# Windowed attention by quarters: 192 score columns a head in place of 256

## The chip, the cores and the metric

The kernel runs on one core of one Trainium2 chip. The metric is the device time of one execution in microseconds (us). Work is spread over TensorE (PE, with its weight loads shown apart as PEld), VectorE (DVE), ScalarE (ACT), GpSimd (POOL) and the DMA queues that SP, ACT and POOL issue to.

## The reference

Attention with a sliding window of 128 keys and 4 sink keys, for 4 batches, 8 heads, 768 positions and head size 64; its output, laid out as 3072 tokens by 512, goes through a highway layer.

```python
pos = np.arange(S)
is_sink = pos[None, :] < int(n_sink)                 # 4
rel = pos[:, None] - pos[None, :]
in_window = (rel >= 0) & (rel < int(window))         # 128
scores = np.where(is_sink | in_window, q @ k.T / sqrt(D), -1e9)
a = softmax(scores)
x = (a @ v) laid out as [3072, 512]
H = np.maximum(x @ w_h, 0.0)
T = 1.0 / (1.0 + np.exp(-(x @ w_t + b_t)))
out = T * H + (1.0 - T) * x
```

A query sees its own key and the 127 before it, and always the first 4 keys of its batch.

## The kernel before

The 3072 tokens are 24 blocks of 128, six to a batch (`NSC` = 6), and each block n goes through a chain of small steps. The order of all steps is written out by hand in `_STEPS`, as `name:block`, and every engine runs its instructions in that order. `_FILLM` puts so many half-size warm-up matmuls ahead of some early steps.

The steps of one block:

- `lq`, `lk`, `lv` (lines 152 to 171): loads of queries, keys and values by POOL's DMA queue, cast from fp32 to fp16 on the way. Blocks 0 to 5 (`PACKED`) load q and k two tokens to a row, into one tile `sp`; the others load plainly, into `qsd` and `ksd`. `v_all` holds the values of block n in 65 columns a head, the last one set to 1, so that the row sums come out of the same matmul.
- `T` (lines 270 to 294): transposes q and k on TensorE, 64 rows at a time; 32 transposes of 64 by 64 for a packed block (line 281), 16 of 64 by 128 for the others (line 291). `cT` copies the result to `qk` on ScalarE (lines 299 and 302).
- `S0`, `S1` (`scores`, line 346): scores of the heads 0 to 3 and 4 to 7, keys on the partitions. For each head there are two matmuls, the 128 keys of the block before and the 128 of its own, against 128 queries: 256 columns a head, or 128 in the first block of a batch. The two heads of a pair lie in the row halves 0-63 and 64-127 and write two different PSUM banks (`sps[:, hh]`).
- `E0`, `E1` (`expo`, line 354): exponential on ScalarE, 1024 columns at a time. `M0`, `M1` (`masked`, line 365): multiplication with a 0/1 mask on VectorE, which brings in the window.
- `sk`, `es`, `BA` (lines 326, 331, 375 and 378): scores of the sink keys, their exponential, and their part of the output. A `sk` serves two blocks. `BA:n` also starts the gate's sum of block n-1 with its bias. Blocks 0 and 1 of a batch have no such step, because the sink keys lie in the window's two key blocks, and their masks (`mask0`, `mask1`) let them through.
- `AV` (line 398): 16 matmuls of 128 keys by 128 queries by 66 columns (8 in a batch's first block), summed in `av`, one PSUM bank for four heads.
- `rec`, `x` (lines 407 and 412): division by the row sums, on VectorE. `X` (line 423) and `cX` (line 434): transposes of the result on TensorE and the copy on ScalarE. `X` uses the PSUM buffer of `av`.
- `Tt`, `u`, `g` (lines 443 to 472): the gate, four matmuls of 512 columns, tanh and scaling. `H`, `d` (lines 459 and 465): the other branch. `ee`, `o` (lines 478 and 484): the mix, and the store by SP's queue.

The last block (`LB`) is done in two halves, with steps named `AVa`, `AVb`, `Xa` and so on (lines 487 to 567). `pks` (line 306) puts the sink keys and values of a batch in place on POOL; `lsv` loads the latter by SP's queue. `pi` and `pm` make the identity and the masks on POOL, and `K0` to `K6` other constants on VectorE.

Of the kernel before, what the change touches and what calls it, by code (L numbers as in the profile page):

```python
# [8 lines left out]
FP16 = mybir.dt.float16  # L9
FP32 = mybir.dt.float32  # L10
AF = mybir.ActivationFunctionType
# [8 lines left out]
_FILL = {'T:5': 1}  # L20
_FILLM = {'T:0': 5, 'T:1': 4, 'S0:0': 1, 'T:2': 9, 'S0:1': 8, 'S1:1': 1, 'AV:0': 1, 'S0:2': 2, 'T:4': 5, 'X:0': 3, 'AV:1': 1, 'S0:3': 2}
_STEPS = """
    K4:0 lq:0 K6:0 lk:0 lk:1 lq:1 K0:0 lk:2 lq:2 pi:0 K3:0 lv:0 lk:4 T:0 cT:0 T:1 pm:0 cT:1
    lsv:0 S0:0 lv:1 lq:4 T:2 K1:0 lk:3 K5:0 lq:3 E0:0 cT:2 S1:0 M0:0 E1:0 S0:1 lw_t:0 lv:2 S1:1
    lbt:0 M1:0 AV:0 E0:1 M0:1 S0:2 E1:1 rec:0 E0:2 K2:0 T:4 x:0 lw_h:0 pks:0 X:0 T:3 cT:4 cX:0
    S1:2 lq:5 lk:5 lv:3 lv:4 lk:6 M1:1 AV:1 rec:1 cT:3 E1:2 x:1 lq:6 S0:3 lq:8 lk:7 lq:7 lk:8
    lv:5 E0:3 sk:2 lk:9 lv:6 lv:7 X:1 sv:0 cX:1 M0:2 M1:2 S1:3 es:2 Tt:0 AV:2 M0:3 BA:2 E1:3
    u:0 S1:4 rec:2 x:2 g:0 S0:4 M1:3 lq:9 Tt:1 H:0 E1:4 X:2 u:1 T:5 E0:4 g:1 H:1 cX:2 cT:5 AV:3
    lk:14 S0:5 d:0 BA:3 M1:4 ee:0 o:0 Tt:2 lk:10 E0:5 u:2 d:1 sk:4 es:4 rec:3 x:3 T:6 X:3 cX:3
    M0:4 cT:6 lv:9 ee:1 S1:5 H:2 AV:4 M0:5 E1:5 BA:4 d:2 S0:6 rec:4 g:2 Tt:3 T:7 x:4 E0:6 o:1  # L30
    M1:5 lsv:6 ee:2 u:3 X:4 cX:4 cT:7 S1:6 H:3 g:3 E1:6 M0:6 AV:5 lq:11 lq:10 S0:7 BA:5 d:3
    E0:7 T:8 cT:8 rec:5 Tt:4 ee:3 S1:7 x:5 X:5 u:4 H:4 cX:5 lv:8 M0:7 M1:6 S0:8 pks:6 lk:11
    lq:12 o:3 lk:12 lv:11 d:4 E1:7 AV:6 E0:8 rec:6 sv:6 Tt:5 x:6 M1:7 T:9 X:6 S1:8 u:5 cX:6 o:2
    g:5 H:5 cT:9 g:4 AV:7 E1:8 S0:9 Tt:6 E0:9 d:5 rec:7 u:6 sk:8 M0:8 T:10 x:7 ee:4 ee:5 M1:8
    X:7 S1:9 es:8 cX:7 g:6 cT:10 H:6 o:4 lv:10 d:6 AV:8 BA:8 S0:10 rec:8 x:8 Tt:7 E1:9 M1:9
    T:11 E0:10 X:8 S1:10 M0:9 H:7 ee:6 u:7 cX:8 cT:11 E1:10 AV:9 o:5 M0:10 BA:9 rec:9 S0:11 d:7
    Tt:8 g:7 sk:10 x:9 E0:11 u:8 T:12 S1:11 X:9 M1:10 M0:11 es:10 cX:9 H:8 cT:12 o:6 AV:10
    E1:11 d:8 BA:10 S0:12 E0:12 rec:10 g:8 x:10 Tt:9 lv:12 lq:13 lk:13 ee:8 M1:11 ee:7 lq:15
    T:13 o:8 X:10 S1:12 H:9 d:9 lq:14 u:9 cX:10 AV:11 lsv:12 lv:13 BA:11 rec:11 cT:13 g:9 lq:18
    x:11 lk:15 E1:12 S0:13 Tt:10 pks:12 lv:14 o:7 lk:16 X:11 ee:9 T:14 M1:12 E0:13 M0:12 M0:13  # L40
    S1:13 u:10 sv:12 cX:11 cT:14 E1:13 H:10 AV:12 rec:12 S0:14 Tt:11 g:10 x:12 lq:16 d:10 M1:13
    X:12 lk:17 E0:14 lq:17 M0:14 T:15 o:9 lv:15 u:11 cX:12 cT:15 S1:14 E1:14 H:11 d:11 AV:13
    rec:13 ee:10 S0:15 g:11 Tt:12 sk:14 x:13 M1:14 T:16 E0:15 lsv:18 u:12 o:10 X:13 S1:15 ee:11
    M0:15 es:14 H:12 o:11 cX:13 AV:14 BA:14 cT:16 rec:14 S0:16 lk:18 E1:15 Tt:13 g:12 E0:16
    T:17 x:14 X:14 d:12 lv:16 u:13 cX:14 S1:16 H:13 M1:15 g:13 M0:16 AV:15 d:13 cT:17 BA:15
    rec:15 E1:16 ee:13 x:15 o:13 ee:12 M1:16 S0:17 E0:17 Tt:14 u:14 o:12 sk:16 T:18 X:15 es:16
    S1:17 lk:19 H:14 lk:20 cX:15 lq:19 AV:16 d:14 lq:21 lv:17 BA:16 cT:18 lq:20 E1:17 lv:18
    rec:16 S0:18 g:14 Tt:15 x:16 M1:17 lk:21 M0:17 E0:18 T:19 pks:18 X:16 u:15 cX:16 S1:18 H:15
    cT:19 M0:18 AV:17 E1:18 BA:17 S0:19 Tt:16 E0:19 sv:18 u:16 lv:19 d:15 rec:17 ee:14 T:20
    lk:22 x:17 M1:18 X:17 g:15 o:14 ee:15 cX:17 H:16 S1:19 g:16 d:16 AV:18 rec:18 lq:22 lv:20  # L50
    lq:23 lv:21 lk:23 lv:22 ee:16 cT:20 E1:19 S0:20 x:18 M1:19 E0:20 Tt:17 T:21 u:17 X:18 cX:18
    M0:19 cT:21 S1:20 H:17 M0:20 o:16 lv:23 AV:19 E1:20 S0:21 Tt:18 d:17 E0:21 sk:20 rec:19
    g:17 x:19 X:19 o:15 u:18 M1:20 M0:21 ee:17 es:20 cX:19 T:22 S1:21 H:18 AV:20 BA:20 d:18
    cT:22 S0:22 Tt:19 g:18 E1:21 E0:22 S1:22 rec:20 ee:18 x:20 M1:21 o:17 M0:22 u:19 X:20 T:23
    cX:20 H:19 g:19 cT:23 d:19 E1:22 AV:21 BA:21 Tt:20 rec:21 sk:22 ee:19 u:20 x:21 es:22 S1:23
    M1:22 o:19 X:21 H:20 cX:21 AV:22 o:18 BA:22 d:20 S0:23 rec:22 E1:23 E0:23 Tt:21 g:20 x:22
    u:21 M1:23 X:22 M0:23 cX:22 ee:20 H:21 d:21 BA:23 AVa:23 AVb:23 Tt:22 g:21 u:22 reca:23
    ee:21 H:22 recb:23 xa:23 xb:23 o:21 Xa:23 g:22 cXa:23 Xb:23 d:22 o:20 cXb:23 TA:23 HA:23
    ee:22 Ta:23 o:22 Hb:23 ua:23 Tb:23 db:23 ga:23 ub:23 Ha:23 da:23 gb:23 eea:23 eeb:23 oa:23
    ob:23  # L60
# [4 lines left out]
def kernel(  # L65
# [31 lines left out]
    VW = H * 65 + 8  # L97
# [14 lines left out]
    NV = NB  # L112
    PACKED = (0, 1, 2, 3, 4, 5)
# [3 lines left out]
    mask = const.tile([P, 2, P], FP16, tag="mask", name="mask")  # L117
    mask0 = const.tile([P, P], FP16, tag="mask0", name="mask0")
    mask1 = const.tile([P, 2, P], FP16, tag="mask1", name="mask1")
# [17 lines left out]
    LB = NB - 1  # L137
# [14 lines left out]
    def load(x, n):  # L152
        if (x, n) in f32:
            eng = nc.sync if x == "q" else nc.scalar
            eng.dma_start(out=f32[x, n], in_=dram(x, n))
        elif x == "v":
            vt = v_all[:, n, :]
            nc.gpsimd.dma_start(  # L158
                out=vt[:, 0:H * 65].rearrange("p (h e) -> p h e", e=65)[:, :, 0:D], in_=dram(x, n))
        elif n in PACKED:  # L160
            if n not in sd_of:
                sd_of[n] = const.tile([P, H, 2 * D], FP16, tag=f"sp{n}", name=f"sp{n}")
            b, c = divmod(n, NSC)
            src = {"q": q, "k": k}[x][b, :, c * P:(c + 1) * P, :]
            i = "qk".index(x)
            nc.gpsimd.dma_start(out=sd_of[n][64 * i:64 * i + 64],
                                in_=src.rearrange("h (p t) d -> p h (t d)", t=2))
        else:
            sd = sd_pool.tile([P, H, D], FP16, tag=f"{x}sd", name=f"{x}sd")
            nc.gpsimd.dma_start(out=sd, in_=dram(x, n))  # L170
            sd_of[x, n] = sd

    def v_cols(n, h):
        return v_all[:, n, 65 * h:65 * h + _AVN]
# [20 lines left out]
    def first():  # L195
        nc.vector.memset(warm, 0.0)  # L196
        nc.vector.memset(ident, 1.0)
        nc.vector.memset(mask, 1.0)
        v_ones(0, NSC)
        warm_up(16)  # L200

    def v_ones(a, b):
        nc.vector.memset(v_all[:, a:b, 0:H * 65].rearrange("p t (h e) -> p t h e", e=65)[:, :, :, D:D + 1], 1.0)
        nc.vector.memset(v_all[:, a:b, H * 65:VW], 0.0)

# [5 lines left out]
    def pm():  # L211
        nc.gpsimd.affine_select(
            out=mask[:, 1, :], in_=mask[:, 1, :], compare_op=ALU.is_ge, fill=0.0,
            base=0, pattern=[[1, P]], channel_multiplier=-1)
        nc.gpsimd.affine_select(
            out=mask[:, 0, :], in_=mask[:, 0, :], compare_op=ALU.is_ge, fill=0.0,
            base=-1, pattern=[[-1, P]], channel_multiplier=1)

    def K1():
        nc.vector.tensor_copy(out=mask0, in_=mask[:, 1, :])  # L220
        nc.vector.memset(mask0[0:NSINK, :], 1.0)
        nc.vector.tensor_copy(out=mask1, in_=mask)
        nc.vector.memset(mask1[0:NSINK, 0, :], 1.0)
# [21 lines left out]
    def K4():  # L245
        v_ones(NSC, NB)
# [21 lines left out]
    avt = {}  # L268

    def T(n):  # L270
        tpf = s_ps.tile([P, 2, DM], FP32, tag="s", name="tp")
        tp = tpf.bitcast(FP16)
        if n in PACKED:
            sd = sd_of.pop(n)
            for j in range(NHP):
                for t in range(2):
                    o = (2 * j + t) * 64
                    for hh in range(2):
                        for i in range(2):
                            rows = slice(64 * i, 64 * i + 64)  # L280
                            nc.tensor.transpose(tp[64 * hh:64 * hh + 64, i, o:o + 64],  # L281
                                                sd[rows, 2 * j + hh, t * D:(t + 1) * D],
                                                ident[rows, rows])
        else:
            qsd, ksd = sd_of.pop(("q", n)), sd_of.pop(("k", n))
            for i, sd in enumerate((qsd, ksd)):
                for j in range(NHP):
                    for a in range(2):
                        rows = slice(64 * a, 64 * a + 64)
                        o = (i * NHP + j) * 64  # L290
                        nc.tensor.transpose(tp[:, a, o:o + 64], sd[rows, 2 * j:2 * j + 2, :],  # L291
                                            ident[rows, rows])
        tp_of[n] = tp

    def cT(n):
        qk = qkT_pool.tile([P, 2 * NHP, P], FP16, tag="qk", name="qk")
        src = tp_of.pop(n)[:, :, 0:DM]
        if n in PACKED:
# [330 lines left out]
```

## Time and profile before

| | |
|---|---|
| median of 3 runs | 114.89 us (114.72 to 117.13) |
| the profiled execution | 114.55 us |
| its span in the profile | 112.5 us |
| TensorE busy | 101.1 us, 1730 matmuls |
| VectorE busy | 94.3 us |
| ScalarE busy | 93.4 us |
| POOL busy | 67.8 us |
| granted TensorE clock, mean | 0.991 |
| loads by POOL's queue | 69792 packets, 10.49 MB |

The span is what the profiler recorded from the first to the last instruction; the time of the execution is 2.05 us longer. Busy time of TensorE is modelled, since its matmuls overlap. A group's line gives the line of the code, the engine, what it writes and reads, the number of instructions, their busy time and the mean duration of one in ns; durations overlap where an engine pipelines, so that a matmul lasts 200 to 400 ns in the records while the next one starts some 30 to 220 ns later.

### The profile page before, as it was taken

To read this page: it belongs to the slowest core of one execution; us is meant where nothing else is said; L and a number is where in the kernel's file an instruction comes from. 1 tells how busy PE (TensorE), PEld (TensorE's weight loads), DVE (VectorE), ACT (ScalarE), POOL (GpSimd) and SP (SyncE) were. 2 spreads that over 40 slices of the span, in tenths; PEclk is the share of its full clock that TensorE was granted. 3 is DMA by queue.
4 is the path that set the end of the run, shared out by engine and by line. 5 is a ranking of instruction groups with operands and counts; after the bars stand their busy time and mean duration, and the time that the engine had idled before them with its cause. 6 is when DMAs were issued, how large, how long until landed. Compare 5 with 4: busy or idle time off the path is not lost.

```text
span 112.5 us, 4097 instructions
## 1 busy us (share of the span) xinstructions
PE 101.1 (90%) x1730; PEld 58.5 (52%) x1730; DVE 94.3 (84%) x225; ACT 93.4 (83%) x131; POOL 67.8 (60%) x93
## 2 busy tenths in 40 slices
PE   5859988979799999999999989999999999999820
PEld 2334555635466555575555546656655666454510
DVE  4314448688589999999999999999999999999980
ACT  4049999978699999999999999999999999783320
POOL 6999996569699599991105999965994000000000
PEclk9999999999999999999999999999999999999996
DMA  0999999999999999999932999999999950240242
GB/s 0 130 150 145 156 162 195 176 154 151 198 160 188 165 176 181 159 207 194 207 116 96 83 166 167 227 192 155 261 160 204 196 136 11 90 187 0 93 187 93
DMA packets 73573, 17.07 MB, mean 152 GB/s; under 512 B 69330, under 2 KB 70610, under 8 KB 73556
## 3 DMA queue, kind: packets, MB, share of 16 engines
q0 software_dynamic: 69792, 10.49, 133.3%
q1 hardware_dynamic: 3620, 6.20, 15.2%
q8 instruction: 13, 0.21, 0.8%
q10 hardware_dynamic: 144, 0.13, 0.3%
q14 instruction: 4, 0.03, 0.1%
HBM read 21.01 MB, written 6.29 MB: 243 GB/s over the span
## 4 chain that ended last, share of the span: by engine, by line
PE 56%; ACT 8%; DVE 1%; issue 1%; DVEq 0%; ACTq 0%
PE hps L459 15%; PE tps L446 13%; PE sps L346 7%; PE av L398 6%; ACT e L354 4%; PE tp L291 4%; PE tps L375 2%; ACT qk L302 2%; PE xtp L423 2%; PE sk L326 1%; PE av L378 1%; ACT u L451 1%; PE tps L443 1%; PE lts L541 1%; PE av L494 1%
## 5 line engine op out<-in xcount | busy, mean ns | idle before, releaser
L354 ACT ACTIVATE e<-sps 128x1024 f16<-128x1024 f32 (+1 forms) x48 | 44.7, 984 | 1.3 <-PE sps L346 1.2
L365 DVE TENSOR_TENSOR e<-e,mask 128x1024 f16<-128x1024 f16 (+1 forms) x48 | 29.4, 635 | 3.0 <-ACT e L354 3.0
L459 PE MATMUL hps<-wh_sb,xT 128*128 128x512 f16 x92 | 23.8, 381 | 0.0
L446 PE MATMUL tps<-wt_sb,xT 128*128 128x512 f16 x92 | 23.8, 381 | 0.0
L158 POOL DMA_DIRECT2D v_all<-in_v_dram x24 | 21.9, 917 | 1.3 <-DMA qsd<-in_q_dram 1.0
L346 PE MATMUL sps<-qk 64*128 64x128 f16 x352 | 17.9, 217 | 1.0 <-ACT qk L299 0.8
L302 ACT COPY qk<-tp 128x1024 f16<-128x1024 f16 x18 | 18.7, 1037 | 0.0
L170 POOL DMA_DIRECT2D ksd<-in_k_dram x18 | 16.5, 926 | 2.2 <-DMA wh_sb<-in_moe_w_h_dram 2.0
L465 DVE SCALAR_TENSOR_TENSOR dd<-hps,xh 128x512 f16<-128x512 f32 x23 | 15.6, 680 | 1.6 <-PE hps L459 1.4
L170 POOL DMA_DIRECT2D qsd<-in_q_dram x18 | 16.3, 914 | 1.2 <-DMA wt_sb<-in_moe_w_t_dram 1.0
L451 ACT ACTIVATE u<-tps 128x512 f16<-128x512 f32 x23 | 14.2, 620 | 3.2 <-PE tps L446 3.1
L412 DVE TENSOR_TENSOR xh<-av,rec 128x512 f16<-128x512 f32 x23 | 15.7, 681 | 0.1
L398 PEld LDWEIGHTS <-e 128*128 128x128 f16 x336 | 13.2, 97 | 4.8 <-DVE e L365 0.6
L484 DVE TENSOR_TENSOR otok<-xh,ee 128x512 f32<-128x512 f16 x23 | 15.6, 681 | 0.1
L346 PEld LDWEIGHTS <-qk 64*128 64x128 f16 x352 | 12.8, 94 | 4.6 <-issue 3.4
L434 ACT COPY xT<-xtp 128x512 f16<-128x512 f16 x23 | 13.7, 598 | 1.3 <-PE xtp L423 1.2
L398 PE MATMUL av<-v_all,e 128*128 128x66 f16 x336 | 14.2, 194 | 0.0
L299 ACT COPY qk<-tp 128x1024 f16<-128x1024 f16 x6 | 7.9, 1317 | 5.7 <-PE tp L281 5.6
L446 PEld LDWEIGHTS <-xT 128*128 128x128 f16 x92 | 7.7, 97 | 8.1 <-issue 0.6
L459 PEld LDWEIGHTS <-xT 128*128 128x128 f16 x92 | 7.2, 98 | 8.0 <-DMA wh_sb<-in_moe_w_h_dram 0.5
L264 PE MATMUL wps<-warm 128*128 128x512 f16 (+1 forms) x33 | 9.9, 414 | 1.3 <-DVE warm L196 1.3
L478 DVE TENSOR_TENSOR ee<-gt,dd 128x512 f16<-128x512 f16 x23 | 9.3, 409 | 0.0
(75 smaller groups left out, 110.4 us busy)
## 6 DMA issues: line engine op xcount, KB each, us to landing
out_dram<-otok SPq DMA_DIRECT2D x23, 256.0 KB, 4.9
v_all<-in_v_dram POOLq DMA_DIRECT2D x24, 128.0 KB, 7.1
ksd<-in_k_dram POOLq DMA_DIRECT2D x18, 128.0 KB, 7.3
qsd<-in_q_dram POOLq DMA_DIRECT2D x18, 128.0 KB, 7.0
sp<-in_q_dram POOLq DMA_DIRECT2D x6, 128.0 KB, 4.6
sp<-in_k_dram POOLq DMA_DIRECT2D x6, 128.0 KB, 4.8
wt_sb<-in_moe_w_t_dram POOLq DMA_DIRECT2D x1, 512.0 KB, 8.4
wh_sb<-in_moe_w_h_dram POOLq DMA_DIRECT2D x1, 512.0 KB, 10.1
```

What stands on the lines that cost most here:

```text
L158: nc.gpsimd.dma_start(out=vt[:, 0:H * 65].rearrange("p (h e) -> p h e", e=65)[:, :, 0:D], in_=dram(x, n))
L170: nc.gpsimd.dma_start(out=sd, in_=dram(x, n))
L302: nc.scalar.copy(out=qk.rearrange("p j (a t) -> p a j t", a=2), in_=src.rearrange("p a (j t) -> p a j t", t=64))
L346: nc.tensor.matmul(sps[:, hh, o:o + P], lhsT=kk[rows, hp, :], rhs=qT[rows, hp, :], start=True, stop=True)
L354: nc.scalar.activation(out=e.rearrange("p a b c d -> p a (b c d)"), in_=sps[:, :, 0:2 * np_ * P], func=AF.Exp, bias=_EXP_BIAS, scale=SCALE)
L365: nc.vector.tensor_tensor(out=ev, in0=ev, in1=m.unsqueeze(1).to_broadcast([P, 4, np_ * P]), op=ALU.mult)
L398: nc.tensor.matmul(av[:, g, 2 * hl + hh, 0:_AVN], lhsT=e[:, hh, hl, pc, :], rhs=v_cols(m, h), start=fresh, stop=False, skip_group_check=True)
L412: nc.vector.tensor_tensor(out=xh.rearrange("p (h d) -> p h d", d=D), in0=av_of.pop(n)[:, :, 0:D], in1=rec_of.pop(n).unsqueeze(2).to_broadc ...
L446: nc.tensor.matmul(t_of[n], lhsT=xT[:, kc, :], rhs=wt_sb[:, kc, :], start=False, stop=(kc == NOC - 1), skip_group_check=True)
L459: nc.tensor.matmul(hps, lhsT=xT[:, kc, :], rhs=wh_sb[:, kc, :], start=(kc == 0), stop=(kc == NOC - 1))
L465: nc.vector.scalar_tensor_tensor(out=dd, in0=h_of.pop(n), scalar=0.0, in1=xh_of[n], op0=ALU.max, op1=ALU.subtract)
L484: eng.tensor_tensor(out=otok, in0=xh_of.pop(n), in1=ee_of.pop(n), op=ALU.add)
```

## The change

A query in the first half of its block sees the keys from 127 before it up to itself. Cut into quarters of 64 keys by 64 queries, two of the eight quarters of a head are masked as a whole: the first 64 keys of the block before against the second 64 queries, and the second 64 keys of the own block against the first 64 queries. The change leaves these out.

- Scores: the 128 columns that all queries need hold the last 64 keys of the block before (partitions 0-63) and the first 64 of the own block (64-127). 64 more columns hold the two triangles: the last 64 own keys by the last 64 queries (0-63), and the first 64 keys of the block before by the first 64 queries (64-127). Each part is a matmul of its own with 64 keys as its stationary operand: 16 for four heads in place of 8. The exponential and the mask have 768 columns in place of 1024.
- Values: `lv` loads windows that are shifted by 64 tokens, 7 a batch (28 in all), the first and the last of half size; 80 columns a head. `AV` becomes 8 matmuls of the full shape, and the triangles are a step of their own, `AX`, with 16 matmuls of 64 keys by 64 queries, which go from one row half to the other output half.
- Sinks: the triangle no longer holds the sink keys for the second half of block 1, so block 1 of each batch gets a `BA` too; there are three `sk` and `es` a batch (the last for one block) in place of two.
- Loads: q and k of blocks 0 to 5 are loaded and transposed as those of the others. `PACKED` is gone.
- Masks: 192 columns, made by four selects on POOL in place of two.
- The order of all steps and the warm-up matmuls are written anew.

The core of the diff:

```diff
-_FILLM = {'T:0': 5, 'T:1': 4, 'S0:0': 1, 'T:2': 9, 'S0:1': 8, 'S1:1': 1, 'AV:0': 1, 'S0:2': 2, 'T:4': 5, 'X:0': 3, 'AV:1': 1, 'S0:3': 2}
+_FILLM = {'T:0': 15, 'S1:0': 10, 'T:1': 4, 'S0:1': 8, 'T:2': 3, 'AX:0': 2, 'S1:2': 2, 'S0:2': 4, 'T:3': 3, 'sk:1': 4}
 _STEPS = """
...
+    lq:1 lq:0 lk:0 lv:0 pi:0 T:0 K4:0 lk:1 lq:2 K6:0 pm:0 lk:2 cT:0 K0:0 lsv:6 S1:0 lbt:0 K1:0
...
+    cX:3 T:6 lv:14 lv:6 H:2 cT:6 lq:8 M0:4 S1:5 M0:5 BA:4 ee:1 lk:13 d:2 Tt:3 AV:4 lk:9 AX:4
...
         elif x == "v":
+            b, j = divmod(n, NW)
+            lo, hi = max(0, j * P - 64), min(S, j * P + 64)
+            r0 = lo - (j * P - 64)
+            vt = v_all[r0:r0 + hi - lo, n, :]
+            nc.gpsimd.dma_start(out=vt.rearrange("p (h e) -> p h e", e=VP)[:, :, 0:D],
+                                in_=v[b, :, lo:hi, :].transpose([1, 0, 2]))
...
     def scores(n, g):
         qT, kT = qkT[n]
-        srcs = ([] if n % NSC == 0 else [qkT[n - 1][1]]) + [kT]
-        np_ = len(srcs)
         sps = s_ps.tile([P, 2, 512], FP32, tag="s", name="sps")
+        if n % NSC == 0:
+            w, parts = P, [(0, kT, 64, 0, 0, P), (64, kT, 0, 0, 0, P)]
+        else:
+            kp = qkT[n - 1][1]
+            w, parts = 192, [(0, kp, 64, 0, 0, P), (64, kT, 0, 0, 0, P),
+                             (0, kT, 64, P, 64, 64), (64, kp, 0, P, 0, 64)]
         for hl in range(2):
             hp = 2 * g + hl
-            for pc, kk in enumerate(srcs):
+            for c0, kk, k0, o, q0, nq in parts:
                 for hh in range(2):
                     rows = slice(64 * hh, 64 * hh + 64)
-                    o = (hl * np_ + pc) * P
-                    nc.tensor.matmul(sps[:, hh, o:o + P], lhsT=kk[rows, hp, :],
-                                     rhs=qT[rows, hp, :], start=True, stop=True)
+                    nc.tensor.matmul(sps[c0:c0 + 64, hh, hl * w + o:hl * w + o + nq],
+                                     lhsT=kk[rows, hp, k0:k0 + 64], rhs=qT[rows, hp, q0:q0 + nq],
+                                     start=True, stop=True)
...
+    def av_full(n, g):
...
+        for hl in range(2):
+            for hh in range(2):
+                nc.tensor.matmul(
+                    av[:, g, 2 * hl + hh, 0:_AVN], lhsT=e[:, hh, hl, 0:P],
+                    rhs=v_cols(v_slot(n, 0), 2 * (2 * g + hl) + hh), start=fresh, stop=False,
+                    skip_group_check=True)
+                fresh = False
+
+    def av_tri(n, g):
+        av, e = avt[n], e_of[n, g]
+        o = 64 if n % NSC == 0 else P
+        for hl in range(2):
+            for hh in range(2):
+                h = 2 * (2 * g + hl) + hh
+                for rows, outs, j in ((slice(0, 64), slice(64, P), 1), (slice(64, P), slice(0, 64), -1)):
+                    if j < 0 and n % NSC == 0:
+                        continue
+                    nc.tensor.matmul(
+                        av[outs, g, 2 * hl + hh, 0:_AVN], lhsT=e[rows, hh, hl, o:o + 64],
+                        rhs=v_cols(v_slot(n, j), h)[rows], start=False, stop=False,
+                        skip_group_check=True)
+
+    def AV(n):
+        for g in range(2):
+            av_full(n, g)
+        done(n)
+
+    def AX(n):
+        for g in range(2):
+            av_tri(n, g)
+        done(n)
```

The new order around two blocks in mid-kernel, TensorE's steps alone: `T:13 BA:10 AX:10 AV:10 Tt:9 S0:13 X:10 H:9 BA:11 T:14 AX:11 S1:13 AV:11 Tt:10 S0:14 X:11 T:15 H:10`. Before: `T:13 X:10 S1:12 H:9 AV:11 BA:11 S0:13 Tt:10 X:11 T:14 S1:13 H:10 AV:12 S0:14 Tt:11`.

## The prediction

> **What bounds the kernel now.** I read the summary of engines and the slices first, then busy time by stretch, the chain that ended last, and the groups of instructions.
>
> ```profile
> PE 101.1 (90%) x1730; PEld 58.5 (52%) x1730; DVE 94.3 (84%) x225; ACT 93.4 (83%) x131; POOL 67.8 (60%) x93
> PE   5859988979799999999999989999999999999820
> ACT  4049999978699999999999999999999999783320
> PEclk9999999999999999999999999999999999999996
> ...
> sum 72.70, PE 72.06 PEld 42.46 DVE 70.67 ACT 69.49 POOL 43.54; mean PE 14.41 PEld 8.49 DVE 14.13 ACT 13.90 POOL 8.71
> ```
>
> The last line is the busy time from 29.4 us (the first transpose of T:6) to 102.1 us (the first matmul of AVa:23). TensorE is idle for 0.64 us there at full granted clock; VectorE and ScalarE stand close behind. As a modelled busy row is no proof, I added up the work. For that I need the price of each step, and of a change of the array's shape between steps. The chain in order of time (start, length, what) shows both:
>
> ```profile
> 84.40 0.32 PE tps L443
> 84.72 0.86 PE tps L446 x4
> ...
> 92.12 0.22 PE sps L346 x8
> 92.34 0.97 PE tps L446 x4
> 93.31 0.33 PE sps L346 x8
> 93.64 0.15 PE xtp L423 x8
> 93.79 0.23 PE tp L291 x16
> 94.02 0.97 PE hps L459 x4
> 94.99 0.49 PE av L398 x16
> 95.48 0.22 PE tps L375
> 95.70 0.12 PE av L378
> ```
>
> The same four gate matmuls cost 0.86 us behind a bias matmul of their own shape (128 rows by 128 columns) and 0.97 behind scores (64 by 128). Eight score matmuls cost 0.22 behind something of shape 64 by 128 and 0.33 behind 128 by 128. So **a change of shape costs 0.11 us**. I count shapes along the step list: transposes T and X, scores S and BA are 64 by 128; AV, Tt and H 128 by 128; sk 128 by 32.
>
> Between T:6 and AVa:23 there are 18 T at 0.23, 37 S (31 at 0.22, 6 for a batch's first block at 0.11), 19 AV (16 at 0.49, 3 at 0.245), 20 X at 0.12, 14 BA at 0.225, 20 H and 19 Tt at 0.86, 6 bias matmuls at 0.22, 6 sk at 0.22: 61.9 us. With 86 changes of shape at 0.11 (9.5) and 0.64 idle that is 72.0 of the 72.7 observed. **TensorE's own instructions and its 86 changes fill this stage.**
>
> The other rows that I draw on:
>
> ```profile
> 5.97 0.45 PE L281 MATMUL tp<-ident,sp 64*64 64x64 f16 x32 [0.67 <-POOL ident L207]
> 6.35 0.60 PE L264 MATMUL wps<-warm 128*128 128x512 f16 x2
> ...
> L354 ACT ACTIVATE e<-sps 128x1024 f16<-128x1024 f32 x40 | 40.2, 1058 | 1.3 <-PE sps L346 1.2
> L365 DVE TENSOR_TENSOR e<-e,mask 128x1024 f16<-128x1024 f16 x40 | 26.4, 679 | 0.6 <-ACT e L354 0.6
> L354 ACT ACTIVATE e<-sps 128x512 f16<-128x512 f32 x8 | 4.9, 616 | 0.0
> L365 DVE TENSOR_TENSOR e<-e,mask 128x512 f16<-128x512 f16 x8 | 3.2, 416 | 2.4 <-ACT e L354 2.4
> ```
>
> The first two (timeline) give the only 64 by 64 tiles of this kernel: 32 transposes take 0.38 us to the next group's start, 0.27 without the change of shape: 34 ns for four, which thus run four at once.
>
> **The change, part by part** (T:6 to AVa:23).
>
> *Exponentials and masks* shrink from 1024 to 768 columns. ScalarE's two forms lie 442 ns apart over 512 columns, VectorE's 263, so 768 columns save about 0.22 and 0.13 us: 0.44 us of ScalarE and 0.26 of VectorE per block. The cover is TensorE, which fills the stage by itself; if it didn't, the saving would be worth up to VectorE's 4 us. All it can give here is TensorE's 0.64 us of idle time: I take -0.3 (0 to -0.64).
>
> *Scores.* Eight matmuls of 64 by 128 become sixteen of 64 by 64: per head pair four with 128 columns, then four with 64. Four at once, as the 64 by 64 transposes, the first four last 0.055 (a pair's time now) and the others 0.034: 0.178 a group in place of 0.22, and 0.11 unchanged for a first block. 31 x -0.042 = -1.3 us. If only two ran at once, it would be 0.36 a group and 0.22 for a first block's, +4.9; the transposes speak against it.
>
> *Values.* AV goes from 16 matmuls to 8 of the full shape: 0.245. The new AX has 16 of 64 by 64 on two tiles that cross (rows 0-63 to outputs 64-127, and the reverse), 66 columns each. As pairs at 31 ns they are 0.245; nothing is saved. In a batch's first block AX is eight on one tile, 0.245, where nothing was before: 3 x 0.245 = +0.7. One by one, AX would be 0.49 in 16 blocks, +3.9. No row has two row halves that write one bank; I take pairs, like L291's two row halves (0.23 for 16).
>
> *Sink part.* Block 1 of each batch gets it too: sk has 10 groups of 16 halves at 0.11 here in place of 6 of 12, +0.4. Three more BA at 0.225 replace three bias matmuls at 0.22: 0. X has one less here by its position, -0.1; T, H and Tt stay.
>
> Sum of work: -1.3 + 0.7 + 0.4 - 0.1 = **-0.3 us**.
>
> *Changes of shape.* Scores were in the shape of T, X and BA beside them; now they and AX have one of their own. Along the new list I count 128 in place of 86: 37 between 128 by 128 and 64 by 128, 36 between 128 by 128 and 64 by 64, 35 between the two 64-row shapes, 20 around sk. 42 x 0.11 = **+4.6 us**. The one place with a change from 64 by 128 to 64 by 64 and no wait (X:2 to T:5) has 0.22 from the start of X to the first transpose of T:5, where eight of them take 0.12: 0.10. Lower end: the 35 cost nothing, +0.8.
>
> *The end.* AVa and AVb hold the same matmul time and three more changes: +0.3.
>
> *The start.* Plain loads take POOL 0.91 to issue, packed ones 0.72: 12 x 0.19 = 2.3 us later for what is behind them, two more mask selects 0.5. A value load of half a window counts 0.72. POOL's list ahead of q:6 (for T:6) is 17 loads at 0.91, a half at 0.72, five selects at 0.25, two weights at 0.8 and pks at 1.2: from its first issue at 1.31 us that is 21.5 us (19.55 before). Such loads land 4.2 us (fastest) or 7.1 us (median) behind their issue, so T:6 could start from 25.7 to 28.6; the 9.8 us of before give 31.3. The bytes ahead of it are half a load fewer, and the slices show about 150 GB/s with either packet size. T:0 waits for the third plain load (issued at 3.1, 4.2 to landing), not for the identity: 7.3 us in place of 5.97, and T:1 to T:4 follow some 2 us late. Against that, ScalarE is the busiest of 10 to 20 us (9.85 of 10) and gets shorter copies (1.04 for 1.32 us) and exponentials. More warm-up matmuls (55 halves for 42, 1.4 us) stand in waits. I take +0.3 (-3.7 to +2). Later loads don't bind: POOL is busy for 43.54 of the stretch's 72.7 us, and 20 whole and 8 half value loads for 24 cost it 2.2 us more in the whole kernel.
>
> Sum: -0.3 - 0.3 + 4.6 + 0.3 + 0.3 = **+4.6 us**. The profiled execution took 114.55 us (span 112.5 and 2.05 around it): 119.15. It lies 0.34 below the median of 114.89, so I say **119.2 us**.
>
> **Rivals.**
>
> *The crossed tiles take turns.* Both halves of an AX pair write one bank of av. In the kernel before, row halves always go to two banks (tp, sps, xtp by a or hh), so nothing speaks for or against. Price: 16 x 0.245 + 0.25 for AVa and AVb = +4.2, **123.4 us**. Chance 0.20. [...]
>
> *The two 64-row shapes change freely.* 35 x 0.11 = 3.85 less: **115.3 us**. Against it stands the one place of 0.10. Chance 0.08.
>
> *The start is shorter (no longer slower than before).* ScalarE is relieved of 6 x 0.28 us for copies and some 2 us of exponentials before T:6, and q:6 lands 4.2 us behind its issue: T:6 starts at 25.7 us rather than 29.4, -3.7 in place of +0.3, **115.2 us**, no change that shows. At 25.1 the whole is level, at 22.8 faster by 2%. For it: TensorE is busy for only 3.3 and 3.2 us of 22 to 26 and 26 to 30 us. Against it: the first blocks' loads come later. Chance 0.21, 0.09 of it for the faster side.
>
> The forecast keeps 0.51, with a range of its own of 116.8 to 121.5.
>
> **How the numbers follow.** Two per cent (2.3 us) is about what a measurement of this kernel tells from no change: 112.6 to 117.2. Slower: 0.20 and 0.48 of the forecast's, 0.68. Same: 0.08, 0.12 of the start's and 0.03 of the forecast's, 0.23. Faster: 0.09. The range takes in the start's lower end and the crossed tiles taking turns: 114.2 to 124.2; some 0.12 lies below and 0.05 above.
>
> **What would show it.** In the changed profile: score groups of 16 at about 0.18 us; AV of 8 at 0.245 and AX of 16 at 0.245 (0.49: the rival); gate matmuls still 0.97 behind a change of shape; T:6 near 29.7 us and from there to AVa about 77 us with TensorE full; ScalarE and VectorE with idle time that ends at TensorE. Wrong, if the stretch is no longer than 73 us, if TensorE shows idle time over 2 us in it, or if the first matmuls behind a change to 64 by 64 come without the 0.1.

## The result and the profile after

| | before | changed |
|---|---|---|
| median on the same chip | 115.12 us (114.72 to 117.13) | 124.07 us (123.71 to 124.67) |
| ratio to before | | 1.080, 95% interval 1.073 to 1.086 |
| profiled execution, its span | 114.55, 112.5 us | 124.22, 122.1 us |
| first transpose of T:6 | 29.37 us | 30.58 us |
| first matmul of AVa:23 | 102.05 us | 111.61 us |
| matmuls | 1730 | 2206 |

The change costs 9 us; the forecast was 4.3. Of the profiled execution's 9.67 us, 8.35 lie between T:6 and AVa:23, 1.2 in the start, and 0.1 behind AVa:23. Where an execution's granted clock dipped it is left out of the ratios here, though not out of the medians.

From the page of the changed kernel, the summary, three rows of slices and the queue that carries instructions (packets, MB, share); then the busy time from 30.6 to 111.6 us:

```profile
PE 108.7 (89%) x2206; PEld 60.2 (49%) x2206; DVE 94.1 (77%) x227; ACT 87.8 (72%) x135; POOL 71.7 (59%) x99
PE   5969878899999999999797896999999999999930
ACT  4038879845998999997699596878889867763420
PEclk9999999999999999999999999999999999999997
q8 instruction: 17, 0.28, 0.9%
```

```profile
sum 81.00, PE 77.46 PEld 43.84 DVE 71.06 ACT 67.83 POOL 45.97; mean PE 77.46 PEld 43.84 DVE 71.06 ACT 67.83 POOL 45.97
```

ScalarE has lost 5.6 us of work, as the change says, and TensorE is idle for 3.54 us of the stretch where it was idle for 0.64. The slices of TensorE show where: 7, 9, 7, 8, 9, 6 in the middle, at full granted clock. The list of what TensorE waited for in this stretch (us in total, times, longest) is three times "issue" and 0.2 us of VectorE, and no transfer:

```profile
PE av L399 <- issue: 1.2, 2, 1.0
PE xtp L437 <- issue: 1.1, 2, 0.8
PE sps L339 <- issue: 1.0, 1, 1.0
```

In the chain that ended last the same idle time stands in the middle of runs of equal matmuls:

```profile
59.86 0.14 PE xtp L437 x2
59.99 0.80 issue
60.79 0.27 PE xtp L437 x6
...
66.31 0.21 PE av L399 x3
66.52 1.01 issue
67.53 0.22 PE av L399 x2
...
73.35 0.18 PE sps L339 x3
73.53 1.02 issue
74.55 0.33 PE sps L339 x13
```

Two of eight transposes of X run, TensorE stands for 0.8 us, then the other six run. All eight read one tile that was complete before the first began, and nothing that the profile shows holds back the third. The same happens in the middle of AX and in the middle of a score group, so the operation isn't the cause. There is no such gap in the stretch before.

I split both stretches by the starts of their matmuls: time in runs of one shape (work), what a change of shape adds, gaps inside a run, and waits at the start of a step.

| us | before | changed | difference | forecast |
|---|---|---|---|---|
| work | 63.4 | 64.4 | +1.0 | -0.3 |
| changes of shape | 87: 8.3 | 129: 12.1 | +3.8 | +4.6 |
| gaps inside runs | 0 | 4.1 | +4.1 | none |
| waits at a step's start | 1.0 | 0.4 | -0.6 | -0.3 |
| sum | 72.7 | 81.0 | +8.35 | +4.0 |

The gaps stand at 53.66, 59.79, 66.33, 73.29 and 79.17 us (0.35, 0.97, 1.17, 1.21 and 0.45 us, counted from start to start less the usual distance). **They are the part that the forecast lacks.**

Counted in the trace's TensorE instructions (each matmul and each weight load is one), the three long gaps begin behind numbers 2239, 2495 and 2751, and the two short ones behind 1983 and 3007: **multiples of 256 apart**. The 17 packets of queue q8 hold 16 KB each, one for some 260 of the 4412 instructions; the kernel before has 13 for 3460. I take it from these counts that q8 carries TensorE's instructions in pieces of 256. Around the three long gaps the trace has such a packet starting at 58.52, 65.26 and 72.13 us, some 25 to 45 instructions before TensorE stands, and TensorE goes on 2.27, 2.28 and 2.42 us after the packet's start. Behind 80 us, when POOL has all but three of its loads issued, there is no gap. This gave the first theory: **TensorE's instructions come in pieces by DMA, the packets stand behind the loads, and a faster use of instructions than before leaves TensorE without any.** In these stretches 256 instructions last 7.4 us in the mean in the kernel before (6.1 at the least), and about 5.4 us in the changed one where it has its gaps, these left out.

### The profile page after: what moved, and what is told of

The parts are those of the page before. It is cut to its first block, busy times and chain, and to the rows that moved or that the text cites. A ratio compares the mean times of both kernels' runs of the same rounds, so it can differ in the third digit from the quotient of the medians.

```text
span 122.1 us, 5067 instructions
## 1 busy us (share of the span) xinstructions
PE 108.7 (89%) x2206; PEld 60.2 (49%) x2206; DVE 94.1 (77%) x227; ACT 87.8 (72%) x135; POOL 71.7 (59%) x99
## 4 chain that ended last, share of the span: by engine, by line
PE 71%; DMA 11%; POOL 7%; issue 4%; DVE 2%; ACT 1%; DVEq 0%; POOLq 0%
PE hps L473 18%; PE tps L460 14%; PE sps L339 9%; DMA wh_sb<-in_moe_w_h_dram 8%; PE av L399 6%; PE av L384 6%; PE tp L284 4%; PE xtp L437 4%; DMA v_all<-in_v_dram 4%; PE tps L367 3%; PE sk L315 2%; POOL qsd L168 2%; POOL ksd L168 2%; PE av L370 2%; POOL v_all L164 1%
## 5 line engine op out<-in xcount | busy, mean ns | idle before, releaser
L348 ACT ACTIVATE e<-sps 128x768 f16<-128x768 f32 (+1 forms) x48 | 37.0, 780 | 3.0 <-PE sps L339 1.7
L357 DVE TENSOR_TENSOR e<-e,mask 128x768 f16<-128x768 f16 (+1 forms) x48 | 24.7, 526 | 2.7 <-ACT e L348 2.6
L168 POOL DMA_DIRECT2D qsd<-in_q_dram x24 | 21.7, 909 | 4.0 <-DMA wh_sb<-in_moe_w_h_dram 1.7
L168 POOL DMA_DIRECT2D ksd<-in_k_dram x24 | 21.5, 898 | 2.0 <-PE av L384 1.0
L339 PE MATMUL sps<-qk 64*64 64x128 f16 (+1 forms) x704 | 18.1, 210 | 1.3 <-issue 1.0
L339 PEld LDWEIGHTS <-qk 64*64 64x64 f16 x704 | 11.7, 106 | 8.9 <-issue 7.5
L421 DVE RECIPROCAL rec<-av 128x8 f32<-128x8 f32 x23 | 4.7, 205 | 13.0 <-PE av L384 7.1
L399 PE MATMUL av<-v_all,e 64*64 64x66 f16 x352 | 11.0, 194 | 1.6 <-issue 1.2
L384 PE MATMUL av<-v_all,e 128*128 128x66 f16 x192 | 10.2, 194 | 0.0
L399 PEld LDWEIGHTS <-e 64*64 64x64 f16 x352 | 8.2, 107 | 3.7 <-issue 2.8
```

Of the source, the lines that this page charges most:

```text
L339: nc.tensor.matmul(sps[c0:c0 + 64, hh, hl * w + o:hl * w + o + nq], lhsT=kk[rows, hp, k0:k0 + 64], rhs=qT[rows, hp, q0:q0 + nq], start=Tru ...
L348: nc.scalar.activation(out=e.rearrange("p a b c -> p a (b c)"), in_=sps[:, :, 0:2 * w], func=AF.Exp, bias=_EXP_BIAS, scale=SCALE)
L357: nc.vector.tensor_tensor(out=ev, in0=ev, in1=m.unsqueeze(1).to_broadcast([P, 4, w]), op=ALU.mult)
L384: nc.tensor.matmul(av[:, g, 2 * hl + hh, 0:_AVN], lhsT=e[:, hh, hl, 0:P], rhs=v_cols(v_slot(n, 0), 2 * (2 * g + hl) + hh), start=fresh, st ...
L399: nc.tensor.matmul(av[outs, g, 2 * hl + hh, 0:_AVN], lhsT=e[rows, hh, hl, o:o + 64], rhs=v_cols(v_slot(n, j), h)[rows], start=False, stop= ...
```

## The experiments

**Scores in 64 by 64 alone** (b_s64), in the kernel before. This adds changes of shape and 352 pairs of instructions, and leaves loads, values, sinks and order as they were.

```diff
-            for pc, kk in enumerate(srcs):
+            for pc, kk, c0 in [(pc, kk, c0) for pc, kk in enumerate(srcs) for c0 in (0, 64)]:
...
-                    nc.tensor.matmul(sps[:, hh, o:o + P], lhsT=kk[rows, hp, :],
+                    nc.tensor.matmul(sps[c0:c0 + 64, hh, o:o + P], lhsT=kk[rows, hp, c0:c0 + 64],
```

> The kernel before with its 256 score columns a head, but each score matmul cut into two of 64 keys (64 by 64), as the changed kernel has them. Nothing else changes; exponentials and masks stay at 1024 columns. By the step list this adds 31 changes of the array's shape between T:6 and AVa:23 (87 to 118) and 352 pairs of weight load and matmul. Theory (a shape of its own costs 0.094 us at each change): +2.9 us in the stretch for the changes and 0.5 to 1 for the first four of each group, 118 to 119 us in all, without stalls inside runs of matmuls. Rival (more instructions on TensorE run its instruction supply dry, about 1 us at a time): 2 to 4 us more than that, 120 to 123 us, with gaps of about 1 us inside runs.

Measured: 120.44 us median, ratio 1.037 (1.027 to 1.047); the profiled execution took 118.89. Its stretch is 75.9 us: 118 changes, 11.1 us; work 64.4; no gap inside a run. 31 changes more cost 2.8 us, so 91 ns each. The changes between the two 64-row shapes are among them and cost the same as the others (93 ns): in the stretch a price of shape changes alone is shown, and that they come for nothing is refuted. Ahead of the stretch the rival is right in one place. TensorE stands in the middle of a run of scores:

```profile
19.58 0.34 PE sps L346 x14
19.92 1.46 issue
21.38 0.24 PE sps L346 x2
```

It goes on 2.33 us after the start of a packet of q8, and T:6 begins at 30.93 us in place of 29.37.

**More instructions, no other shape** (b_split), in the kernel before: each gate matmul of 512 columns becomes four of 128.

```diff
-            nc.tensor.matmul(hps, lhsT=xT[:, kc, :], rhs=wh_sb[:, kc, :],
-                             start=(kc == 0), stop=(kc == NOC - 1))
+            for c in range(4):
+                cols = slice(P * c, P * c + P)
+                nc.tensor.matmul(hps[:, cols], lhsT=xT[:, kc, :], rhs=wh_sb[:, kc, cols],
+                                 start=(kc == 0 and c == 0), stop=(kc == NOC - 1), skip_group_check=True)
...
```

> The kernel before, each gate and highway matmul of 512 columns (lines 446 and 459) cut into four of 128. TensorE gets 552 pairs of weight load and matmul more (1730 to 2282, the changed kernel has 2206); shapes and their changes stay as they are, and the columns too. By the rows 128 columns take 56 ns, four 223 for 216: +1.2 us in all. Theory (the supply of instructions to TensorE, in pieces of 16 KB, is what stalled the changed kernel inside its runs): gaps of 0.3 to 1.3 us inside runs while loads fill the DMA queues, 2 to 5 us in all, 118 to 121 us. Rival (the stalls come with the crossed or small tiles and not with the number of instructions): 116 us and no gap over 0.3 us inside a run.

Measured: 119.09 us median, ratio 1.036 (1.026 to 1.046). The stretch is 77.3 us with the 87 changes of before, work 64.45, and 4.2 us of gaps inside runs, the largest 0.75, 1.27 and 1.68 us at 33.7, 56.7 and 79.3 us. From its chain:

```profile
56.73 0.14 PE tp L291 x2
56.87 1.10 issue
57.97 0.38 PE tp L291 x14
```

These transposes are the very ones of the kernel before, where they run without a gap. The three large gaps begin behind numbers 1215, 2239 and 3262, again multiples of 256 apart (within one record). They come with the number of instructions, without AX, scores in quarters or the changed loads.

**Less work for ScalarE and VectorE alone** (b_relief), in the kernel before: exponential and mask on 768 of 1024 columns. The value matmuls read other columns in place of those left out.

```diff
-                             in_=sps[:, :, 0:2 * np_ * P], func=AF.Exp,
+                             in_=sps[:, :, 0:2 * w], func=AF.Exp,
...
```

> The kernel before with exponential and mask on 768 of the 1024 columns of a group; a quarter of the score columns is left out of the exponential, and the value matmuls read other columns in their place. TensorE's instructions are those of before. Theory (TensorE is the bound): within 1 us of before, since TensorE was idle for 0.64 us of 72.7 there. Rival (VectorE and ScalarE, 97 and 96% busy in that stretch, set the pace too): 2 to 4 us faster.

Measured: 114.9 us median, ratio 0.991 (0.985 to 0.997). The stretch of the profiled execution is no shorter (73.2 us, TensorE busy for 72.28). The relief of ScalarE and VectorE is worth about 1 us by the ratio: TensorE has to get through the same list.

**The changed kernel without the loads of batches 1 to 3** (a_noload): they take the rows of batch 0.

```diff
         elif x == "v":
             b, j = divmod(n, NW)
+            if b:
+                return
...
-            sd = sd_pool.tile([P, H, D], FP16, tag=f"{x}sd", name=f"{x}sd")
-            nc.gpsimd.dma_start(out=sd, in_=dram(x, n))
-            sd_of[x, n] = sd
+            if n < NSC:
+                kept[x, n] = const.tile([P, H, D], FP16, tag=f"{x}sd{n}", name=f"{x}sd{n}")
+                nc.gpsimd.dma_start(out=kept[x, n], in_=dram(x, n))
+            sd_of[x, n] = kept[x, n % NSC]
```

> The changed kernel without the loads of q, k and v of batches 1 to 3; they compute with batch 0's tiles. TensorE's, VectorE's and ScalarE's instructions and their order stay. Theory (a fetch of instructions is late because the loads' packets are ahead of it on the DMA engines): the gaps inside runs (4.1 us between 53 and 80 us) are gone and the whole is 4 to 6 us shorter than the changed kernel's 124.07, the start's own waits for loads included. Rival (the fetch takes its 2.3 us whatever else the queues do, and dense runs outrun it): gaps of about 1 us remain, and the whole is 0 to 2 us shorter.

Measured: 119.2 us in the profiled execution (121.27 median), 5.0 less than the changed kernel's. Every TensorE instruction and change of shape is that of the changed kernel, and the gaps are gone: 129 changes (12.1 us), work 64.3, waits 0.4. The busy time of its stretch:

```profile
sum 76.80, PE 76.57 PEld 43.50 DVE 69.46 ACT 67.58 POOL 2.20; mean PE 76.57 PEld 43.50 DVE 69.46 ACT 67.58 POOL 2.20
```

**b_split without the later loads** (b_splnl), the case that completes a table of two by two: the later blocks take the rows of earlier ones.

```diff
         elif x == "v":
+            if n >= NSC:
+                return
...
-            sd = sd_pool.tile([P, H, D], FP16, tag=f"{x}sd", name=f"{x}sd")
-            nc.gpsimd.dma_start(out=sd, in_=dram(x, n))
-            sd_of[x, n] = sd
+            if n < 2 * NSC:
+                kept[x, n] = const.tile([P, H, D], FP16, tag=f"{x}sd{n}", name=f"{x}sd{n}")
+                nc.gpsimd.dma_start(out=kept[x, n], in_=dram(x, n))
+            sd_of[x, n] = kept[x, NSC + n % NSC]
```

> The kernel before with Tt's and H's gate matmuls in four quarters of 128 columns (as in b_split), and without the loads of q and k of batches 2 and 3 and of v of batches 1 to 3: these blocks take the rows of earlier ones. Theory (instructions reach TensorE late because their pieces stand behind loads): 3400 or more instructions are as harmless as in the kernel before once the loads are gone: no gap inside a run from 50 us on (before that some loads are left), T:6 to AVa:23 72.7 to 74 us, 114.5 to 116 us in all. Rival (quarters cost something of their own, or TensorE takes instructions more slowly whatever else goes on): the 4 us of b_split stay, 118.5 to 119.5 us.

Measured: 116.38 us median, ratio 1.013 (1.003 to 1.022); stretch 73.6 us, work 64.45 as in b_split. One gap of 0.75 us is left, at 34.2 us, while loads still run; none behind it. The quarters themselves cost the 1 us of work. Gaps inside runs, in us:

| | loads as they are | without the later loads |
|---|---|---|
| before (1730 matmuls) | 0 | not run |
| b_split (2282) | 4.2 | 0.75 |
| changed (2206) | 4.1 | 0 |

In these runs it takes both the loads and the faster use of instructions. b_s64, with 2082 matmuls and all loads, had none in its stretch, where 256 instructions last 6.3 us in the mean, and the one of 1.46 us ahead of it.

**The same loads, issued later** (a_late). The bytes stay; only the order of the list changes (q and k from block 8 and the values five blocks ahead of use, and five buffers in place of eight, so that POOL can't run ahead).

```diff
-    sd_pool = ctx.enter_context(tc.tile_pool(name="p_sd", bufs=8))
+    sd_pool = ctx.enter_context(tc.tile_pool(name="p_sd", bufs=5))
...
-    cX:3 T:6 lv:14 lv:6 H:2 cT:6 lq:8 M0:4 S1:5 M0:5 BA:4 ee:1 lk:13 d:2 Tt:3 AV:4 lk:9 AX:4
+    lv:7 x:3 X:3 E0:5 cX:3 T:6 lk:11 lv:6 H:2 cT:6 M0:4 S1:5 lq:10 M0:5 BA:4 ee:1 d:2 Tt:3 AV:4
```

> The changed kernel with the same loads, but metered: five tiles each for q and k in place of eight, and the three loads of block n+5 behind the steps of block n (from block 8 on). TensorE's instructions are the same. Theory (the fetch of instructions is late because up to eight loads are queued on the DMA engines; 8 x 0.9 us is about the delay): with about three queued, the gaps inside runs shrink from 4.1 us to under 1 us, and the whole is 3 to 4 us shorter than the changed kernel's, 120 to 121 us. Rival (any traffic of loads delays the fetch by a few us, however it is spread): gaps of 3 us or more stay, 123 to 125 us.

Measured: 129.23 us median, ratio 1.121 (1.112 to 1.131): a miss as a remedy. With five buffers POOL waited 11.0 us in all for transposes, T:6 began at 34.4 us, AX waited 3.1 us for a value window, and the granted clock was at half for 6.8 us from 47.3 us on. At full clock no gap inside a run was left, though; the cure had worked where it was not hidden by its own cost.

**Fewer changes of shape** (a_group): `T:k` moved to `X:k-4` and `S0:k` to `S1:k-1`, for k from 8 to 22. **Both together** (a_both). TensorE's steps alone:

```diff
-S0:13 X:10 H:9 BA:11 T:14 AX:11 S1:13 AV:11 Tt:10 S0:14
+X:10 T:14 H:9 BA:11 AX:11 S1:13 S0:14 AV:11 Tt:10
...
```

> The changed kernel in another order from block 8 to 22: S0 of a block stands directly behind S1 of the block before and AX, and T beside X, so that steps of one shape stand together; 114 changes of shape between T:6 and AVa:23 in place of 128. Same instructions and loads. Theory (0.094 us a change): -1.3 us in the stretch, with the gaps inside runs as in the changed kernel or a little longer, since TensorE gets through its instructions faster: 122 to 124 us. Rival (the order, not the number of changes, sets the pace through the PSUM buffers): TensorE waits on cT or E, and the whole is over 125 us.

> The changed kernel with both: metered loads, and the order that has 14 changes of shape fewer. Theory: the two add up, 3 to 4 and 1.3 us, 118.5 to 120 us, which is still slower than the kernel before. Rival (one of the two undoes the other): 121 us or more.

Measured: 131.24 us (1.144, 1.136 to 1.151) and 136.81 us (1.190, 1.183 to 1.198). Both fell to their rivals. The 14 changes saved 1.1 us (115 for 11.0 us), and TensorE then waited: in a_group 3.0 us for exponentials and 1.3 for copies of transposes that now had to be done earlier, since S1, S0 and T share two PSUM buffers:

```profile
PE sps L339 <- ACT e L348: 3.0, 10, 0.3
PE sps L339 <- ACT qk L291: 1.3, 3, 0.8
```

The order with its many changes of shape is the price of giving ScalarE time between the steps; a_both adds its own 3.6 us wait for a value window. In neither is "issue" among the waits of the stretch: with the loads of the changed kernel, but a slower use of instructions (a span of 129.0 us in place of 122.1 for the same 2206 matmuls), a_group has no such gap either.

**Plain loads alone** (b_plain), in the kernel before: `PACKED = ()`.

```diff
-    PACKED = (0, 1, 2, 3, 4, 5)
+    PACKED = ()
```

> The kernel before with plain loads and transposes of q and k for blocks 0 to 5 too, as the changed kernel has them; all else as before. It tells what this part does to the start. Theory (plain loads cost POOL 0.19 us more each, 2.3 us in all, and the first blocks come 1 to 2.5 us later, but the start is then held by the bytes of the loads): T:6 starts 0.5 to 2 us later than the 29.4 us of before, 115.5 to 117 us in all. Rival (ScalarE's shorter copies, 6 x 0.28 us, make up for it): within 0.5 us of before.

Measured: 117.63 us, ratio 1.025 (1.019 to 1.030). T:0 begins at 7.16 us in place of 5.97, T:6 at 29.96 in place of 29.37. The rest lies in the stretch, 75.7 us with 2.6 us of gaps; the profile's waits there are 1.3 us for VectorE ahead of X, 0.7 for a q load and 0.7 for a value load. The order of before isn't made for these loads and the changed kernel has another, so this part can't be added to the others; of the changed kernel's start it accounts for 0.6 of 1.2 us, and the other 0.6 stays open.

**Loads paced without a cost at the start** (a_pace): q and k from block 8 on have four buffers of their own and are listed four blocks ahead, as are their value windows; the first eight blocks' loads stay. **The same with two value windows put first** (a_pace2).

```diff
+    late_pool = ctx.enter_context(tc.tile_pool(name="p_late", bufs=4))
...
-            sd = sd_pool.tile([P, H, D], FP16, tag=f"{x}sd", name=f"{x}sd")
+            sd = (sd_pool if n < 8 else late_pool).tile([P, H, D], FP16, tag=f"{x}sd", name=f"{x}sd")
```

> The changed kernel with the loads of q and k from block 8 on, and their value windows, listed four blocks ahead of their use and with four buffers of their own, so that they can't run ahead; the first eight blocks' loads as they were. Same matmuls and changes of shape. Theory (pieces of instructions stand behind bunched loads): gaps inside runs fall from 4.1 us to less than 1.5, T:6 to AVa:23 77 to 79 us, 120 to 121.5 us in all; still slower than the kernel before by the changes of shape, the work and the start. Rival 1 (TensorE is short of instructions at this rate whatever the loads do in detail): 4 us of gaps stay, 124 us. Rival 2 (values and keys now come late): the gaps turn into waits for DMA at a step's start, 123 us or more.

> As a_pace, with the value windows of blocks 6 and 7 issued ahead of the later keys and queries: in a_pace they came late, and TensorE stood 4.0 us at 42.3 us and ran at a lower clock behind it, while no gap inside a run was left from 50 us on. Theory (pieces of instructions stand behind bunched loads, and that is all that the 4.1 us were): no wait over 1 us, gaps inside runs under 1.5 us in all, T:6 to AVa:23 77 to 78.5 us, 120 to 121.5 us in all. Rival 1 (gaps come back once TensorE isn't held up by the late values, because it then uses instructions faster than they come): 3 to 4 us of gaps, 123.5 to 124.5 us. Either way slower than the kernel before.

Measured for a_pace: 125.96 us, ratio 1.099 (1.086 to 1.112). No gap inside a run from 51 us on, but the value window of AX:6 was issued at 40.4 us behind later keys; TensorE waited for it and ran at half the clock for 3.4 us from 47.1 us on:

```profile
PE av L400 <- DMA v_all<-in_v_dram: 5.2, 3, 3.9
```

For a_pace2, with only that order mended: **120.54 us median (119.23 to 123.47), ratio 1.037 (1.030 to 1.044)**, against 1.080 of the changed kernel. What TensorE waited for from 32.0 to 108.8 us, and the busy time there:

```profile
PE xtp L438 <- DVE xh L427: 0.2, 1, 0.2
```

```profile
sum 76.80, PE 76.56 PEld 43.48 DVE 70.48 ACT 67.58 POOL 43.73; mean PE 76.56 PEld 43.48 DVE 70.48 ACT 67.58 POOL 43.73
```

The same 1698 matmuls as in the changed kernel, the same loads, all bytes: 76.8 us in place of 81.0, with 129 changes at 12.1 us, work 64.3, and no gap inside a run. (T:6 at 32.0 us is later than in the changed kernel; the clock was at 0.6 to 0.7 in two slices before it.) What differs is when POOL issues: in a_pace2 its loads come in groups, with waits of 0.9 to 2.5 us for the transposes between them. From 50 to 80 us the changed kernel issues 27 loads and a_pace2 26, but they stand in the queue for less long. From the transfers of that time, the changed kernel first (packets, MB and the packets' time as a share of 16 engines' span; then count, size and median us from issue to landing):

```profile
q0 software_dynamic: 29320, 3.69, 193.8%
...
qsd<-in_q_dram POOLq DMA_DIRECT2D x9, 128.0 KB, 7.7
```

```profile
q0 software_dynamic: 25695, 3.24, 170.4%
...
qsd<-in_q_dram POOLq DMA_DIRECT2D x8, 128.0 KB, 5.4
```

That the loads make TensorE's own instructions late is shown by what the runs change: taking the loads away, or only spacing them, removes the gaps with every matmul in place. The packets say what is late. I counted where each one starts, in TensorE instructions behind the last of the multiples above. In the stretch of a_noload that is from 24 ahead to 56 behind: a packet starts about when TensorE enters a piece of 256. In the changed kernel the packets ahead of the five gaps start 176, 212, 228, 230 and 154 behind, and those ahead of the three large gaps of b_split 162, 221 and 218. Within their stretches no packet starts later than 116 behind in a_pace2, 142 in b_s64 and 135 in the kernel before, and none of these has a gap there. The packets themselves last 0.88 to 1.12 us in the changed kernel and 0.88 to 1.51 us in a_noload, so it is their start that is late. An estimate from these figures agrees: at 47 instructions a us, the 2.3 us from a packet's start to TensorE's going on are 108 instructions, which leaves 148 of 256 as the latest start without a gap.

That the packet waits in the DMA, and not its request ahead of it, was not tested by itself; nor are the loads' bytes separated from POOL's issuing of them, since a_noload takes away both and a_pace2 spaces both. How full the queue must be isn't settled either: the kernel before shows 6.7 to 7.5 us to landing in the same time and no gap, at its slower use of instructions (7.4 us for 256). No version beats the kernel before: without gaps the changed order still carries 3.8 us of shape changes and 1 us of work more.

## Why the prediction was right and wrong

- **The step that failed: the part on waits.** It took TensorE's idle time to be what other engines left of it, saw 0.64 us of it, and gave -0.3. It never asked what feeds TensorE with instructions, although it counted 476 matmuls more and the page before had a queue for them. It also wrote that later loads don't bind because POOL has time to spare; they did bind, by way of the instructions. Rows of before showed no gap, so the rate (256 instructions in 7.4 us in the mean) passed unnoticed as a margin. Worth +4.1 us, nearly all of the miss. The bound that was named, idle time over 2 us in the stretch, has been passed (3.54).
- **The price of a change of shape** was forecast as 0.11 us and is 94 ns (84 to 99 for nearly every pair of shapes). The count held: 42 more. +3.8 for +4.6.
- **Scores and values** together: about +0.2 in place of -0.6, and the scores are what failed. By starts a group that stands between other shapes takes 0.21 us where 0.178 was forecast (0.235 before, for 0.22). The four matmuls that run at once start 4 ns apart, but behind a change the second four start 80 ns behind the first, not 55; the later fours follow after 28 to 59 ns. The 64 by 64 transposes were too kind a row.
- **The other work**: the sinks +0.5 for +0.4, BA +0.3 for 0, X +0.1 for -0.1. The work came to +1.0 for -0.3. With the cheaper changes and the waits these errors cancel: a_pace2 and a_noload have 76.8 us in the stretch, the forecast 76.7. That agreement is luck; the terms were off by about 1 us either way.
- **The start** took 1.2 us more and not 0.3, 0.6 of it with the plain loads alone; the rest is not explained.
- **The rival of the crossed tiles is refuted.** From the chain of the changed kernel:

```profile
78.73 0.30 PE sps L339 x16
79.03 0.34 PE tp L284 x16
...
100.62 0.25 PE av L399 x16
100.87 0.35 PE av L384 x8
```

AX takes 0.25 us for its 16 matmuls without a change of shape in front: its pairs start 4 ns apart and the next pair 30 ns later, though both halves write one bank of av. One by one it would have been 0.49, by the time of AV's 16 matmuls in the kernel before (an estimate). The time came out near this rival's 123.4, for another reason: only the parts tell them apart.
- **The rival of free changes between the 64-row shapes is refuted** by the same rows: T lasts 0.34 behind scores of 64 by 64, and 0.23 behind X, whose shape is that of T.
- **The rival of the shorter start** fell too: T:6 began 1.2 us later, not 3.7 earlier.
- **ScalarE and VectorE** shrank as forecast (groups of the changed kernel; 1058 and 679 ns before), and by itself it bought little, as the forecast had said (about 1 us in b_relief, for 0.3):

```profile
L348 ACT ACTIVATE e<-sps 128x768 f16<-128x768 f32 x40 | 32.3, 817 | 2.4 <-PE sps L339 1.3 <-ACT qk L291 1.0
...
L357 DVE TENSOR_TENSOR e<-e,mask 128x768 f16<-128x768 f16 x40 | 21.5, 548 | 1.6 <-ACT e L348 1.6
```

## What to carry to other kernels

A matmul cut into small ones was paid three times here: in changes of shape (42 more, 3.8 us), in the second four of a score group, which started 80 ns behind the first where 55 were forecast, and in instructions: 476 matmuls more, with 4.1 us of gaps inside runs beside the loads as they were and none beside the loads of a_pace2. Where idle time named "issue" stands inside a run of equal matmuls, count instructions between the gaps and look at what loads are under way; spacing the loads (fewer buffers, or a list nearer to their use) gave back 4.2 us of 81.0 in the stretch here with every matmul in place. But a load listed late at one place cost about as much as all the gaps did (a_pace): 3.9 us of waiting for one value window, and 3.4 us at half the granted clock behind it.

## What was not expected of the hardware

- At about 47 instructions a microsecond, while the loads of 50 to 80 us took 7.3 to 7.7 us (medians) to land, TensorE stood in the middle of runs: 0.97 to 1.21 us a time at three places, behind instructions that are multiples of 256 apart, 4.1 us in all with two short ones. Each long gap ended 2.3 to 2.4 us after the start of a 16 KB instruction packet, which had started 212 to 230 instructions behind the last of those multiples. Without the later loads (a_noload), or with them spaced (a_pace2), the same matmuls ran without a gap.
- A wait of 3.1 us on TensorE, from 45.4 us on, came with 6.8 us at half the granted clock from 47.3 us on (a_late); one of 3.9 us, from 42.3 us on, with 3.4 us from 47.1 us on (a_pace). By an estimate, half of that time behind the wait, 2.7 and 1.7 us, is lost on top of it.
- In AX of the changed kernel two 64 by 64 tiles that cross, and write one PSUM bank, started 4 ns apart, and the next pair some 30 ns later: 0.25 us for 16.
